# HGRN2 attention and a gated MLP on one core: new group sizes and priorities, and all transposes on TensorE in place of twenty by DMA

## The chip, the cores and the metric

The kernel runs on one core of a Trainium2 chip. The metric is the device time of one execution in microseconds (us), the median of several runs. The kernel before has a median of 213.93 us over 3 runs (213.22 to 216.14).

## What is computed

The inputs are q, k, v and f_logit of shape (4, 8, 768, 48): batch, heads, tokens, head size, all fp32. A gated linear recurrence over the tokens is followed by a two-layer MLP with the activation h * cos(h):

```python
f = 1.0 / (1.0 + np.exp(-f_logit))
for t in range(S):
    state = f[:, :, t, :, None] * state + einsum('bhd,bhe->bhde', k[:, :, t], v[:, :, t])
    y[:, :, t] = einsum('bhd,bhde->bhe', q[:, :, t], state)
x = y.transpose(0, 2, 1, 3).reshape(B * S, H * D)     # 3072 x 384
h = x @ w_in                                          # 384 x 2048
out = (h * np.cos(h)) @ w_out                         # 2048 x 384, fp32
```

## The kernel before

**Chunks.** The 768 tokens of each batch row are cut into chunks of 128, so there are 24 chunks, numbered n = 0 to 23, six to a batch row. Within a chunk the recurrence is done with matmuls, and a state of 48 x 48 per head goes from one chunk to the next of the same row. For every chunk:

- f, k, q and v are loaded by SyncE's DMA queue (`load`, L392-403). The first `NPAIR = 4` chunks put two neighbouring tokens in one partition, in two DMAs of 96 KB (L399), the others take one DMA of 192 KB (L396). The q of chunk 0 is issued by ScalarE's queue.
- `decay` (L413-473) turns f into the cumulated gates: exp (L422) and ln (L437) on ScalarE, cumulated sums by matmuls with a triangle of ones (L448-463), then two exp (L468), which give b and bi. One call serves one chunk or two.
- `attend` (L475-634): qk = q * b and k * bi (L482, GpSimd; VectorE too for n < 4), v cast to bf16 (L389). qk is transposed into qkt. For most chunks this is eight TensorE transposes into one PSUM bank (L511 for paired chunks, L515 for the others) and a copy out of it by VectorE or ScalarE (L525, "qkt"). For n in `TURN_QK` it is one DMA transpose on SyncE's queue (L517), with no PSUM and no copy. Then scores (L541, L550), the causal mask (am, L554, VectorE), the state's product (L570, L575), the state's update (st L584 VectorE, sz L590 GpSimd), y from the state and from the scores (L600, L607, L612), and its cast to bf16 (yb, L525). yb is transposed into xT: three TensorE transposes (L630) and a copy (xT, L525), or for n in `TURN_Y` one DMA transpose on SyncE's queue (L622).
- `moe` (L638-690) works on units of 128, 128, then 256 tokens (`UNITS`): h = xT against w_in (L651, 6 matmuls for each half of a 1024-column PSUM tile), cos on ScalarE (L658), gT = h * cos on VectorE (L661), then w_out (L671, 16 matmuls of 384 columns for 128 tokens), a copy to SBUF (ot, L674) and a store by SyncE (L682, L685).

**Weights.** w_in and w_out come in four pieces each of 768 KB fp32 on SyncE's queue (`load_weights`, L371-386). Each is staged in a slot of the gT pool and cast to bf16 by VectorE, ScalarE or GpSimd (L389), whichever the planner finds free.

**PSUM.** Eight banks serve three kinds of request, whose banks overlap: pairs of banks for h (L350) and for scores (L351), single banks for all else (L352: transposes, y, state products, o). A bank is free for the next request when its last reader is done.

**Who sets the order.** Nothing runs in the order of the Python loops. Each piece of work is an `op` with an engine (or several, with a cost for each), the values it reads and writes, and a priority from the table `PR`. `Plan.run` (L155-245) places the ops one after another on planned engine times: among those that can start about now, the lowest priority number goes first. It thus chooses the engine of every copy and cast, the PSUM bank and buffer of every value, and the order on every engine, SyncE's queue among them. Each engine then executes its list strictly in that order.

`GROUPS` lists the chunks that share a stretch of exp and ln on ScalarE: exp/ln and sin lie in different activation tables, and while a group is open no cosine may be placed. A number is the chunks of one `decay` call. `PR["gate"][g]` holds group g's first exp back until so many cosines are planned:

```python
for o, g in gates:
    if PR["gate"][g] is not None:
        o.deps.add(cosines[PR["gate"][g] - 1])
```

From group 1 (`FREE_GROUPS = 1`) on, the first exp waits until all f pieces of its group are loaded. The table load ahead of an exp group is shown at L737, that ahead of cosines at L658.

Of the kernel before, what the change touches and what calls it, by code (L numbers as in the profile page):

```python
# [116 lines left out]
class Plan:  # L117
# [37 lines left out]
    def run(self):  # L155
# [11 lines left out]
        while len(order) < n:  # L167
# [77 lines left out]
        return order  # L245


GROUPS = [(1, 1, 1), (1,), (2,), (2, 2), (2, 2), (2, 2), (2, 2), (2,)]
UNITS = [128, 128] + [256] * 11
NPAIR = 4  # L250
FREE_GROUPS = 1
TURN_QK = range(14, 23)
TURN_Y = range(12, 23)
PR = {
    "at": [-12.29, -6.15, -7.86, -3.54, -3.92, 15.62, -19.28, -37.09, -8.89, 2.67, 9.58, 17.38, 9.92, 20.25,
          -11.32, -1.58, 13.93, 10.35, 34.42, 26.02, 40.51, 24.64, 16.95, 12.68],
    "dec": [-8.47, -57.31, -61.04, -69.2, -28.24, -49.14, -79.64, -48.44],
    "f": [-43.16, -25.03, -22.97, -8.07, -2.31, -6.19, 24.79, 54.63, 17.72, 57.23, 51.15, 47.24, 55.46,
          53.45, 44.74, 80.64, 54.13, 111.71, 112.22, 68.31, 95.05, 72.38, 86.37, 55.7],
    "h": [3.03, 31.23, 1.72, -0.8, 2.61, 9.56, -7.84, 18.41, -24.77, 18.52, 17.84, 12.56, -12.9],  # L260
    "k": [-21.87, -16.94, -7.69, -4.47, -9.06, 6.14, 15.33, 36.65, 25.42, 15.32, 15.8, 44.24, 49.16, 72.37,
          75.37, 80.56, 68.29, 83.23, 95.28, 87.29, 95.57, 100.98, 97.99, 79.82],
    "o": [58.13, 26.04, 22.05, 54.64, 24.66, 21.51, 44.13, 47.06, 68.58, 102.72, 70.22, 82.65, 82.73],
    "tq": [1.37, -18.62, 8.94, -41.89, -22.72, -30.79, -29.34, 13.32, 0.45, 25.45, 44.49, 73.32, 0.51, 38.11,
          -19.6, -35.07, -26.72, -52.99, -63.88, -22.16, -23.59, 5.62, -39.1, -8.27],
    "ty": [-29.44, -2.23, -1.14, -18.62, -50.77, -26.99, -41.9, -38.55, -40.26, -17.32, 25.61, -2.03, 2.74,
          8.38, 49.55, 45.48, 2.91, -0.4, -39.16, -44.82, -2.61, -2.74, -26.93, -15.21],
    "v": [-26.8, -34.27, -11.26, 0.13, 3.34, 10.3, 16.09, 22.38, 43.81, 38.01, 48.41, 44.56, 41.68, 43.68,
          90.07, 49.48, 98.02, 44.19, 100.52, 65.78, 64.72, 77.22, 79.02, 126.2],
    "w_in": [-45.54, -7.28, 5.66, -12.05],  # L270
    "w_out": [6.72, 10.57, 101.81, 165.61],
    "wc": [0.78, -2, -17.61, -40.6, -45.98, 2.72, 16.43, 45.54],
    "gate": [None, None, 1, 1, 5, 20, 28, 36],
}


def build(nc, cpool, ppool, q, k, v, f_logit, moe_w_in, moe_w_out, out):
# [79 lines left out]
    def act(n, src="P", ptr=False):  # L357
        return 0.833 * n + (160 if src == "P" else 198) + (95 if ptr else 0) - 55

    def dve(n, rate=1.04):  # L360
        return rate * n + 153 - 55
# [113 lines left out]
    def attend(b, c, n, ld, bt, bi, i, prio):  # L475
# [28 lines left out]
        def tr(e):  # L504
# [8 lines left out]
            for j in range(2):  # L513
                for p in range(NP):
                    nc.tensor.transpose(out=o[:, j * NP + p, :], in_=pair(j, p), identity=ident)  # L515
        if n in TURN_QK:
            P.op("tq", {"SP": 420.0}, lambda e: nc.sync.dma_start_transpose(  # L517
# [6 lines left out]
        def cp(e, o, i_):  # L524
            (nc.scalar.copy if e == "ACT" else nc.vector.tensor_copy)(out=o, in_=i_)  # L525
        if n not in TURN_QK:
            P.op("qkt", {"DVE": dve(1024, 0.52), "ACT": act(1024)}, lambda e: cp(
# [92 lines left out]
        x = xT[n]  # L620
        if n in TURN_Y:
            P.op("ty", {"SP": 420.0}, lambda e: nc.sync.dma_start_transpose(out=x.ap, in_=yb.ap),  # L622
# [70 lines left out]
    n, t0, units = 0, 0, list(UNITS)  # L693
    for g, group in enumerate(GROUPS):
        at0 = n
# [74 lines left out]
```

## Time and profile before

| | |
|---|---|
| runs of the kernel | 213.22, 213.93, 216.14 us; median 213.93 |
| the profiled execution | 213.22 us, span of the core 211.4 us |
| granted TensorE clock | 0.984 of full speed |
| busy: TensorE / its weight loads | 174.7 / 130.2 us |
| busy: VectorE / ScalarE / GpSimd | 137.8 / 130.5 / 68.7 us |
| L671 (w_out) and L651 (w_in) matmuls | 70.1 and 69.8 us, 384 and 624 of them |
| L661 (g) / L658 (cosines) / L554 (am) | 57.9 / 52.9 / 29.3 us |
| activation table loads | 14, 1283 ns each |
| DMA | 33.62 MB, mean 159 GB/s; 106560 of 113237 packets under 512 B |
| DMA transposes on SyncE's queue | 9 of qk, 11 of yb |

The span goes from the first to the last instruction of the core; the time of the execution is 1.8 us longer. "Busy" is time in which an engine executed; matmuls overlap, so a matmul's own duration is longer than its share of the path. In the rows of a profile, PE is TensorE, PEld its weight loads, DVE VectorE, ACT ScalarE, POOL GpSimd, and SPq SyncE's DMA queue. L512 is line 512 of the kernel. A row `out<-in` names the tiles by the program's names; all PSUM tiles are called ps. A wait is put down to what ended it.

### The profile page before, as it was taken

To read this page: it belongs to the slowest core of one execution; us is meant where nothing else is said; L and a number is where in the kernel's file an instruction comes from. 1 tells how busy PE (TensorE), PEld (TensorE's weight loads), DVE (VectorE), ACT (ScalarE), POOL (GpSimd) and SP (SyncE) were. 2 spreads that over 40 slices of the span, in tenths; PEclk is the share of its full clock that TensorE was granted. 3 is DMA by queue.
4 is the path that set the end of the run, shared out by engine and by line. 5 is a ranking of instruction groups with operands and counts; after the bars stand their busy time and mean duration, and the time that the engine had idled before them with its cause. 6 is when DMAs were issued, how large, how long until landed. Compare 5 with 4: busy or idle time off the path is not lost.

```text
span 211.4 us, 4701 instructions
## 1 busy us (share of the span) xinstructions
PE 174.7 (83%) x1871; PEld 130.2 (62%) x1871; DVE 137.8 (65%) x179; ACT 130.5 (62%) x157; POOL 68.7 (32%) x108
## 2 busy tenths in 40 slices
PE   0152685678989888999989899999998999989983
PEld 0142574566757745787847657768875678857651
DVE  1825859798858963679882776845896767814400
ACT  2274279867994865295887635689687455815511
POOL 8300114820073134486007751119051711000000
PEclk9999599999999999999999999999999999999999
DMA  6969799999998988979988999845955241011113
GB/s 186 181 168 229 192 228 249 271 245 239 274 180 176 198 169 195 219 167 214 177 170 183 182 221 173 175 128 101 145 111 139 64 86 41 0 52 39 40 39 112
DMA packets 113237, 33.62 MB, mean 159 GB/s; under 512 B 106560, under 2 KB 111680, under 8 KB 113216
## 3 DMA queue, kind: packets, MB, share of 16 engines
q1 hardware_dynamic: 112672, 33.14, 71.8%
q10 hardware_dynamic: 544, 0.20, 0.5%
q8 instruction: 14, 0.23, 0.5%
q14 instruction: 7, 0.06, 0.1%
HBM read 25.17 MB, written 4.72 MB: 141 GB/s over the span
## 4 chain that ended last, share of the span: by engine, by line
PE 50%; DVE 7%; ACT 1%; issue 1%; DVEq 0%; ACTq 0%
PE ps L671 23%; PE ps L651 20%; DVE gT L661 3%; PE ps L612 1%; PE ps L550 1%; ACT ot L674 1%; DVE am L554 1%; DVE st L584 1%; PE ps L458 1%; PE ps L600 1%; PE ps L575 1%; DVE yb L525 1%; DVE qkt L525 1%; PE ps L515 1%; PE ps L630 1%
## 5 line engine op out<-in xcount | busy, mean ns | idle before, releaser
L671 PE MATMUL ps<-w_out_bf,gT 128*128 128x384 bf16 x384 | 70.1, 326 | 6.8 <-DVE st L584 2.1
L651 PE MATMUL ps<-xT,w_in_bf 128*128 128x256 bf16 (+1 forms) x624 | 69.8, 264 | 4.1 <-DVE w_in_bf L389 2.3
L661 DVE TENSOR_TENSOR gT<-ps,cosh 128x1024 bf16<-128x1024 f32 x48 | 57.9, 1219 | 14.7 <-ACT cosh L658 14.2
L658 ACT ACTIVATE cosh<-ps,halfpi 128x1024 bf16<-128x1024 f32 x48 | 52.9, 1113 | 23.1 <-PE ps L651 19.5
L651 PEld LDWEIGHTS <-w_in_bf 128*128 128x128 bf16 x624 | 55.9, 98 | 12.4 <-DVE w_in_bf L389 2.5
L671 PEld LDWEIGHTS <-gT 128*128 128x128 bf16 x384 | 35.6, 97 | 29.0 <-issue 8.5
L482 POOL TENSOR_TENSOR qk<-q,b 128x384 bf16<-128x384 f32 x21 | 21.1, 1004 | 38.1 <-ACT b L468 23.0
L590 POOL TENSOR_TENSOR sz<-st,b 64x192 bf16<-64x192 f32 x32 | 16.1, 503 | 33.1 <-DVE st L584 30.0
L554 DVE TENSOR_TENSOR am<-ps,umask 128x1024 bf16<-128x1024 f32 x20 | 24.4, 1218 | 2.9 <-ACT bi L468 1.3
L482 POOL TENSOR_TENSOR qk<-k,bi 128x384 bf16<-128x384 f32 x20 | 20.4, 1021 | 2.8 <-DMA k<-in_k_dram 2.4
L674 ACT COPY ot<-ps 128x384 f32<-128x384 f32 x16 | 7.7, 478 | 21.8 <-PE ps L671 16.7
L422 ACT ACTIVATE f<-f 128x768 f32<-128x768 f32 (+1 forms) x14 | 10.1, 747 | 9.7 <-DMA f<-in_f_logit_dram 9.6
L468 ACT ACTIVATE b<-ps 128x776 f32<-128x776 f32 (+1 forms) x14 | 10.2, 729 | 8.8 <-issue 4.6
L389 DVE CAST w_in_bf<-gT 128x1536 bf16<-128x1536 f32 x4 | 7.0, 1752 | 9.2 <-DMA gT<-in_moe_w_in_dram 9.2
L584 DVE TENSOR_TENSOR st<-ps,sz 128x384 f32<-128x384 f32 x16 | 8.8, 552 | 5.3 <-PE ps L575 2.4
L525 DVE CAST yb<-ps 128x384 bf16<-128x384 f32 x14 | 7.8, 554 | 6.6 <-PE ps L671 2.1
L389 POOL CAST vb<-v 128x384 bf16<-128x384 f32 x9 | 4.5, 503 | 20.3 <-PE ps L612 16.5
L448 PE MATMUL ps<-sp,incl 128*128 128x384 bf16 x4 | 2.0, 501 | 10.7 <-ACT sp L437 10.7
L468 ACT ACTIVATE bi<-ps 128x768 f32<-128x768 f32 (+1 forms) x14 | 10.1, 723 | 0.7 <-PE ps L511 0.7
L737 ACT ACT_TABLE_LOAD x7 | 9.0, 1283 | 2.2 <-issue 2.1
L437 ACT ACTIVATE sp<-f 128x768 bf16<-128x768 f32 (+1 forms) x14 | 10.0, 744 | 0.1
L389 DVE CAST vb<-v 128x384 bf16<-128x384 f32 x11 | 5.9, 535 | 5.3 <-PE ps L612 5.2
(68 smaller groups left out, 174.5 us busy)
## 6 DMA issues: line engine op xcount, KB each, us to landing
k<-in_k_dram SPq DMA_DIRECT2D x20, 192.0 KB, 4.2
q<-in_q_dram SPq DMA_DIRECT2D x20, 192.0 KB, 4.1
f<-in_f_logit_dram SPq DMA_DIRECT2D x20, 192.0 KB, 4.1
v<-in_v_dram SPq DMA_DIRECT2D x20, 192.0 KB, 3.7
out_dram<-ot SPq DMA_DIRECT2D x20, 192.0 KB, 2.7
gT<-in_moe_w_in_dram SPq DMA_DIRECT2D x4, 768.0 KB, 5.5
gT<-in_moe_w_out_dram SPq DMA_DIRECT2D x4, 768.0 KB, 7.3
f<-in_f_logit_dram SPq DMA_DIRECT2D x8, 96.0 KB, 3.1
```

The costliest lines, as they stand in the source:

```text
L389: (nc.scalar.copy if e == "ACT" else nc.vector.tensor_copy if e == "DVE" else nc.gpsimd.tensor_copy)(out=o, in_=i_)
L422: first = P.op("exp", {"ACT": act(384 * m, "S")}, lambda e: nc.scalar.activation(out=fl(ft.ap), in_=fl(ft.ap), func=AF.Exp, scale=-1.0), r ...
L468: nc.scalar.activation(out=out_.ap[:, 0:m, :], in_=i, func=AF.Exp, scale=s)
L482: lambda e, j=j, src=src, dec=dec: E(e).tensor_mul(out=qk.ap[:, j, :, 0:D].rearrange("p (e h) d -> p h e d", e=2) if pm else qk.ap[:, j, : ...
L525: (nc.scalar.copy if e == "ACT" else nc.vector.tensor_copy)(out=o, in_=i_)
L554: P.op("am", {"DVE": dve(1024)}, lambda e: nc.vector.tensor_mul(out=am.ap.rearrange("p r a n -> p (r a n)").rearrange("p (a n) -> p a n", ...
L584: P.op("st", {"DVE": dve(384)}, lambda e: nc.vector.tensor_add(out=st.ap, in0=pv(), in1=S_in.ap), reads=[ps, S_in], writes=[st], prio=prio)
L590: eng().tensor_mul(out=S_out.ap[s, :, r, :], in0=srcap()[s, :, r, :], in1=bt.ap[s, i, HD:, None].broadcast_to([64, NP, D]))
L651: nc.tensor.matmul(ph.ap[:, g * T:(g + 1) * T], lhsT=w_in_bf[:, m, f0:f0 + 128], rhs=x[:, m, :], start=(g % (G // 2) == 0 and m == 0), sto ...
L658: nc.scalar.activation(out=co.ap, in_=ph.ap, func=AF.Sin, bias=halfpi),
L661: P.op("g", {"DVE": dve(1024)}, lambda e, ph=ph, co=co, gv=gv: nc.vector.tensor_mul(out=gv.ap, in0=ph.ap.rearrange("p (g t) -> p g t", t=T ...
L671: nc.tensor.matmul(po.ap[:, 0:d_model], lhsT=gT.ap[:, j, i * C:(i + 1) * C], rhs=w_out_bf[:, j, :], start=(j == 0), stop=(j == KF - 1))
```

## The change

Only constants at the top of the file change; all functions stay as they are.

- `GROUPS`: the first four chunks form one group, where there were three and one. There are seven groups in place of eight; the calls of `decay` keep their sizes (four of one chunk, ten of two).
- `TURN_QK` and `TURN_Y` become empty: no transposes go by DMA. All 24 chunks take the branches at L520-529 and L625-634.
- `PR`: every priority and every gate has a new value. With them the planner lays down a new order on every engine, and other engines for some copies and casts.

```diff
-GROUPS = [(1, 1, 1), (1,), (2,), (2, 2), (2, 2), (2, 2), (2, 2), (2,)]
+GROUPS = [(1, 1, 1, 1), (2,), (2, 2), (2, 2), (2, 2), (2, 2), (2,)]
 UNITS = [128, 128] + [256] * 11
 NPAIR = 4
 FREE_GROUPS = 1
-TURN_QK = range(14, 23)
-TURN_Y = range(12, 23)
+TURN_QK = range(0)
+TURN_Y = range(0)
 PR = {
...
-    "w_in": [-45.54, -7.28, 5.66, -12.05],
-    "w_out": [6.72, 10.57, 101.81, 165.61],
-    "wc": [0.78, -2, -17.61, -40.6, -45.98, 2.72, 16.43, 45.54],
-    "gate": [None, None, 1, 1, 5, 20, 28, 36],
+    "w_in": [-18.28, -18.39, -16.82, -44.7],
+    "w_out": [15.05, 28.06, 93.44, 75.18],
+    "wc": [11.41, 20.66, 14.9, -38, -7.48, 26.57, 33.33, -29.29],
+    "gate": [None, 1, 1, 9, 28, 1, 40],
```

The other rows of `PR` ("at", "dec", "f", "h", "k", "o", "tq", "ty", "v") change in all their numbers too. In the built program the instructions on the engines differ as follows; those not named are as many as before, though in another order:

| engine | instruction | before | after |
|---|---|---|---|
| TensorE | qk transposes L515 | 88 | 160 |
| TensorE | yb transposes L630 | 39 | 72 |
| VectorE | copies qkt / xT / yb / ot | 9 / 8 / 14 / 8 | 15 / 19 / 8 / 11 |
| VectorE | casts of w_in, of v (whole chunks); qk products | 4, 11; 7 | 1, 10; 6 |
| ScalarE | copies qkt / yb / ot | 6 / 10 / 16 | 9 / 16 / 13 |
| ScalarE | casts of w_in / of w_out | 0 / 1 | 3 / 0 |
| GpSimd | casts of v (whole chunks) / of w_out; qk products | 9 / 0; 41 | 10 / 1; 42 |
| SyncE's queue | DMA transposes | 20 | 0 |

SyncE's queue at the start, before: w_in piece 1, f0, v0, v1, f1, f2, k0, k1, q1, w_in 2, v2, k4, q4, f3, k2, q2, w_in 3, f4, k3, q3, f5, v3, v4, w_in 4, k5, q5, w_out 1. After: w_in 1, f0, f1, f2, v0, k0, k1, q1, v1, w_in 2, w_in 3, w_in 4, k2, f3, q2, k3, q3, v2, f4, v4, v3, f5, k4, q4, v5, k5, q5, w_out 1. (The number is the chunk's.)

## The prediction

> **What bounds the kernel now.** I read the page's busy times and slices first, then a table of busy time by stretch, then the chain of waits, then the timeline of the start. The page:
>
> ```profile
> span 211.4 us, 4701 instructions
> ...
> PE 174.7 (83%) x1871; PEld 130.2 (62%) x1871; DVE 137.8 (65%) x179; ACT 130.5 (62%) x157; POOL 68.7 (32%) x108
> ...
> PE   0152685678989888999989899999998999989983
> ...
> DMA  6969799999998988979988999845955241011113
> ...
> PE 50%; DVE 7%; ACT 1%; issue 1%; DVEq 0%; ACTq 0%
> ```
>
> PE leads, and its idle time lies at the left edge. The DMA engines are nearly full until about slice 28 (148 us). The table by stretch (first PE, weight loads, DVE, ACT and POOL, then clock, DMA share, GB/s) puts numbers on it:
>
> ```profile
> 0.00:57.00 57.00, 31.85 (x430) 26.15 (x431) 38.40 (x59) 34.82 (x47) 17.33 (x41) 0.94 0.94 225
> 60.00:120.00 60.00, 54.18 (x597) 40.12 (x595) 43.53 (x59) 41.44 (x49) 28.39 (x38) 1.00 0.91 186
> 120.00:185.00 65.00, 63.67 (x668) 47.63 (x667) 48.64 (x56) 43.41 (x47) 22.17 (x30) 1.00 0.60 117
> 185.00:212.00 27.00, 22.01 (x150) 14.37 (x147) 5.83 (x5) 8.28 (x12) 0.00 (x0) 0.99 0.16 55
> ```
>
> PE is idle 25.2 us in the first 57, 5.8 us from 60 to 120, and only 1.3 us from 120 to 185. The last is the stretch whose transposes go by DMA. So from 120 us on one more microsecond of PE work is a microsecond of span, and DVE (75%) and ACT (67%) have room. The chain of waits, in order of time, shows at what pace short matmuls really pass:
>
> ```profile
> 102.32 0.45 PE ps L515 x8
> 102.77 0.78 PE ps L671 x4
> ...
> 109.57 0.17 PE ps L630 x3
> ```
>
> A single transpose is listed with 219 ns, but eight of them take 0.45 us of the path and three take 0.17 us: they overlap. The DMA transposes that take their place late in the kernel:
>
> ```profile
> L517 SPq DMA_TRANSPOSE qkt<-qk x9: 1232/1309/2777, 116.0 to 170.0; - x9
> ```
>
> That is 9 of qk; 11 more, of yb, have a median of 1190 ns on SyncE's queue. They land after 3.6 and 2.9 us. The start, from the timeline:
>
> ```profile
> 19.11 1.75 DVE L389 CAST w_in_bf<-gT 128x1536 bf16<-128x1536 f32 x1 [2.42 <-DMA gT<-in_moe_w_in_dram]
> ...
> 22.50 0.52 ACT L422 ACTIVATE f<-f 128x384 f32<-128x384 f32 x1 [3.49 <-DMA f<-in_f_logit_dram]
> ...
> 25.07 0.56 DVE L482 TENSOR_TENSOR qk<-q,b 128x384 bf16<-128x384 f32 x1 [0.32 <-DMA q<-in_q_dram]
> ...
> 27.97 1.75 DVE L389 CAST w_in_bf<-gT 128x1536 bf16<-128x1536 f32 x1 [1.87 <-DMA gT<-in_moe_w_in_dram]
> ```
>
> Each cast or product starts as its transfer lands, so these rows date the transfers: a 768 KB weight piece takes about 3.0 us (27.97 - 25.07, with a little waiting), a 192 KB chunk piece of the paired kind about 1.03 us (the f pieces started exp at 7.56 and 11.68 us, four transfers apart).
>
> **What the Trainium skill says.** TensorE: Matmul & The Clock Gate, "Part 4: PE-mode transpose": a PE transpose goes to PSUM and so needs a copy after it, and took about 275 ns inside one kernel. This trace has 219 ns listed, and 56 ns of pace, which decides. VectorE: DVE Perf Modes, "The three transpose paths": TensorE where PSUM will do, 1309 ns for a 128x128 by DMA. Here one instruction of eight blocks issues in 1309 ns and lands in 3.6 us, so that figure isn't a cost per block here. Perfetto Trace Analysis, "Identifying the Most-Contended Engine": matmul busy time does not tell the distance to roofline. Agreed (weight loads are busy 62%); I use it only to say that PE is never without queued work. The same page, "Optimization Strategy": repeated bubbles can mean that PSUM or SBUF has run out. The waits of PE from 60 to 120 us are of this kind.
>
> **The change part by part.** The title speaks of loads, weights and PSUM, but the pairing of four chunks, the SyncE weight queue and the PSUM code stand in both programs. What differs, by the built order, is this.
>
> *Transposes moved to PE.* TURN_QK and TURN_Y become empty. SP loses 9 + 11 DMA transposes; PE gains 72 + 33 matmuls and as many weight loads. 9 x 0.45 + 11 x 0.17 = 4.05 + 1.87 = 5.9 us, all between chunks 12 and 22, which is from about 105 us on, where PE has no gaps. I take +5.9. Zero would need gaps that aren't there; unpipelined (219 ns each) it would be 23 us, which the chain rows exclude.
>
> *Evictions.* DVE: qkt +6 x 0.69, xT +11 x 0.36, yb -6 x 0.56, ot +3 x 0.55, w_in casts -3 x 1.75, one vb and one qk less (-1.3): -0.2 us in sum. ACT: w_in casts +3 x 1.47 (the row of its one weight cast), minus that one cast, qkt +3 x 1.01, yb +6 x 0.48, ot -3 x 0.48: +7.4. POOL: one qk (1.0), one vb (0.5), one weight cast (about 4 x 0.5, an estimate by elements from the vb row): +3.5 of 68.7. None becomes the bound: ACT would be at 138 of some 217 us. PE's own matmuls hide these; what they can cost is order and banks. 20 more requests for single PSUM banks stand in the late stretch, among those of o, y and ps. PE waits in order, so behind an L671 that waits for an xT copy stands all of PE. From 60 to 120 us, where all transposes go by PE, the table of PE's waits lists 1.3 us of L671 behind xT copies and 0.6 us behind yb copies, 1.9 in 60 us. Over 65 us: +2.1. Bounds: 0 (the order was planned anew) and 5.0 (the whole idle rate of 60 to 120 in place of that of 120 to 185: (5.82/60 - 1.33/65) x 65).
>
> *SyncE's queue.* 9 x 1.31 + 11 x 1.19 = 25 us of issue time fall away, with waits of the queue for qk and yb in which loads and stores stood behind. That is worth little: PE was idle 1.3 us there, so no load was late for it.
>
> *The start.* Chunk 3 joins the first group, and the queue's order changes. The same bytes stand ahead of w_in's second piece, so it lands at 19.1 as before; the third and fourth follow at once, at 22.1 and 25.1 (before: 28.0 and 37.3). Behind them chunk 3's f lands at 27.2 (22.5), chunk 2's q at 28.2 (25.1), its v at 31.3, then three pieces, with chunk 3's v at 34.2. On ACT, which casts the three pieces now: cast of the fourth ends at 26.6; exp and ln of chunk 3 at 28.3; its sums on PE 0.9, b and bi 1.0, table load 1.28: 31.5. First cosine 1.11: 32.6 (before: 33.1). Then comes a cast of chunk 3's v, at the head of ACT's queue, so to 34.7; second cosine, 35.8; table 37.1; exp, ln, sums, b, bi of the next group 3.9 us; table 42.2; six cosines 6.6, two qkt 2.0, a yb 0.5: the next table load is at 51.3, after eight cosines. Before it was at 53.46, after seven. That is 2.2 + 1.1 = 3.3 us ahead. Some 1.3 us of it I expect to lose to small waits among the cosines (the row before had 1.0 beside the one for a weight). So -2.0. Bounds: -5.0 (also without PE's 2.3 us of waits for w_in casts) and +3.0 (chunk 2's q is 3.1 us later, and DVE now has a cast of chunk 1's v, landing near 14.8, ahead of chunk 0's k product, which started at 13.5). Table loads stay seven of each kind, so the merged group saves none.
>
> *Sum.* 211.4 - 2.0 + 5.9 + 2.1 = 217.4 us of span. The profiled execution took 213.22, 1.8 more than its span: 219.2. That execution is 0.7 below the median of the three runs, 213.93; I put the forecast between, 219.5, 2.6% above the median.
>
> **The rivals.**
> *The start pays it back.* The start gains 5.0 and the stalls stay at 1.0: 213.2 - 5.0 + 5.9 + 1.0 = 215.1. For: all of w_in is in place 12 us earlier. Against: PE waited only 2.3 us for its casts, and chunks 2 and 3 come later.
> *Evictions stall PE.* Copies and PSUM banks are what PE waits for late, at the full 5.0, and the start loses 2.0: 213.2 + 5.9 + 5.0 + 2.0 = 226.1. For: ACT has 7.4 us more, and head-of-queue waits for v at 14.8, 31.3 and 34.2. Against: in the kernel before DVE and ACT are under 80% busy in each of these stretches.
> *Faster: the start's idle time is filled.* Of PE's 25.2 idle us before 57, more than 12 vanish because MoE units 0 and 1 run straight through on early weights: 213.2 + 5.9 + 2.1 - 12 = 209.2. It decides from a gain of 11.6 us on (209.6 is 2% under the median). Against: 8.7 of these 25 us precede the first matmul, which waits for f, and f comes no earlier.
>
> **How the numbers follow.** Forecast 0.52 (its own range 217 to 222.5), start pays 0.22, evictions stall 0.20, faster 0.06. Two per cent, 209.7 to 218.2, is about what a measurement of this kernel can tell from no change. Of the forecast's case 0.10 lies under 218.2; so slower 0.42 + 0.20 = 0.62, same 0.10 + 0.22 = 0.32, faster 0.06. The range leaves out the faster case and the ends of the others: 214.5 to 226.
>
> **What would show it.** Right: PE busy near 181 us, idle of 22 to 24 us before 57; eight L515 still at 0.45 us in the chain; the idle of PE after 120 us at 3 to 4 us and ended by copies of xT, qkt or yb; second cosine near 35 us, and eight cosines before the third exp table. The start's step is wrong if PE has done less than 32 us of work by 57, or over 37. The stall step is wrong if the late stretch stays at 1.3 us idle, or goes over 6. The transpose step is wrong if PE's busy time grows by less than 4 us.

## The result, and the profile after

The changed kernel takes 227.2 us in the median of four runs (226.43 to 227.31), beside 215.03 for the kernel before on the same chip: 1.056 times the time, 95% interval [1.047, 1.066]. The forecast was 219.5, with a range to 226. The profiled execution took 227.23 us, with a span of 225.4: 14.0 more than before, where the forecast's sum had 6.0. A profile shows one execution, and that of before (213.22) is the fastest of its four: by the medians the difference is 12.2. So up to 2 of the 14.0 us that follow may belong to the two executions and not to the change.

The lines of the page that answer to those shown of before, with the row of the granted clock:

```profile
span 225.4 us, 4908 instructions
...
PE 187.4 (83%) x1976; PEld 140.9 (62%) x1976; DVE 138.2 (61%) x188; ACT 137.8 (61%) x165; POOL 71.8 (32%) x111
...
PE   0327876699999579799999898989999999998883
...
PEclk9999999679999958999999999999999999999999
DMA  6979899999989999995120189791010100111011
...
PE 58%; DVE 12%; ACT 6%; issue 5%; POOL 0%; DVEq 0%; ACTq 0%
```

PE is busy 12.7 us longer, not 5.9. It has a new hole in slices 14 and 15 (73 to 85 us), and its clock dips twice, to half speed (slices 8 and 9, and slices 15 and 16). The transfers, full until about 100 us, then fall away for some 25 us and come back. DVE and ACT are in the chain with 18% where they had 8%. The table by stretch (columns as in the prediction) is cut, from 57 us on, where the two programs part. First after:

```profile
0.00:57.00 57.00, 35.89 (x415) 28.67 (x416) 35.36 (x60) 31.98 (x41) 19.68 (x42) 0.94 0.93 229
57.00:75.00 18.00, 16.79 (x186) 12.30 (x185) 12.45 (x19) 16.88 (x19) 6.35 (x7) 1.00 0.94 191
75.00:105.00 30.00, 24.98 (x300) 20.15 (x297) 19.56 (x26) 19.54 (x24) 16.02 (x22) 0.89 0.93 189
105.00:225.40 120.40, 109.73 (x1088) 79.74 (x1085) 70.79 (x85) 69.37 (x83) 29.72 (x40) 1.00 0.27 67
```

Then before, with the same cuts; its first row stands in the prediction:

```profile
57.00:75.00 18.00, 16.20 (x168) 11.84 (x165) 13.99 (x19) 13.94 (x18) 7.06 (x8) 1.00 0.92 186
75.00:105.00 30.00, 27.70 (x330) 21.22 (x327) 21.27 (x30) 18.35 (x25) 14.97 (x20) 1.00 0.90 189
105.00:211.40 106.40, 98.96 (x956) 71.03 (x948) 64.17 (x73) 63.35 (x72) 29.30 (x39) 1.00 0.54 111
```

Read the last rows first. At 105 us after has 109.73 us of PE work left where before had 98.96: 10.8 more. From there on PE idles 120.4 - 109.7 = 10.7 us, before 7.4: 3.2 more, with rounding. Together these are the 14.0 us. The added transposes, 105 at 56 ns and all after 105 us, are 5.9 of the 10.8. The other 4.9 I call lag: PE work that before had behind it by then. Most of it is w_out matmuls. Counted from the trace, both kernels have issued 288 L651 by 105 us, but before 100 L671 and after 80; 20 at 0.163 us is 3.3. The rest was not traced to single instructions. At 75 us after had been ahead: 192 L651 in both, and 64 L671 to 56. The lag arises between 75 and 105 us.

### The profile page after: what moved, and what is told of

Same layout as the page of the kernel before. It is cut to its first block, busy times and chain, and to the rows that moved or that the text cites. A ratio compares the mean times of both kernels' runs of the same rounds, so it can differ in the third digit from the quotient of the medians.

```text
span 225.4 us, 4908 instructions
## 1 busy us (share of the span) xinstructions
PE 187.4 (83%) x1976; PEld 140.9 (62%) x1976; DVE 138.2 (61%) x188; ACT 137.8 (61%) x165; POOL 71.8 (32%) x111
## 4 chain that ended last, share of the span: by engine, by line
PE 58%; DVE 12%; ACT 6%; issue 5%; POOL 0%; DVEq 0%; ACTq 0%
PE ps L651 24%; PE ps L671 23%; PE ps L515 3%; PE ps L550 2%; DVE am L554 2%; DVE st L584 2%; ACT qkt L525 2%; PE ps L630 2%; DVE gT L661 2%; DVE qkt L525 2%; PE ps L612 1%; ACT cosh L658 1%; PE ps L600 1%; DVE yb L525 1%; DVE vb L389 1%
## 5 line engine op out<-in xcount | busy, mean ns | idle before, releaser
L671 PE MATMUL ps<-w_out_bf,gT 128*128 128x384 bf16 x384 | 71.3, 328 | 7.2 <-ACT qkt L525 2.5
L651 PE MATMUL ps<-xT,w_in_bf 128*128 128x256 bf16 (+1 forms) x624 | 74.5, 275 | 0.5 <-DVE xT L525 0.4
L651 PEld LDWEIGHTS <-w_in_bf 128*128 128x128 bf16 x624 | 59.1, 102 | 10.1 <-issue 1.0
L671 PEld LDWEIGHTS <-gT 128*128 128x128 bf16 x384 | 35.9, 98 | 29.2 <-issue 9.5
L674 ACT COPY ot<-ps 128x384 f32<-128x384 f32 x13 | 6.2, 479 | 16.4 <-PE ps L671 13.9
L468 ACT ACTIVATE b<-ps 128x776 f32<-128x776 f32 (+1 forms) x14 | 10.1, 729 | 9.6 <-PE ps L461 4.4
L525 DVE COPY qkt<-ps 128x1024 bf16<-128x1024 bf16 x15 | 10.3, 688 | 7.8 <-PE ps L575 2.7
L674 DVE COPY ot<-ps 128x384 f32<-128x384 f32 x11 | 6.0, 554 | 13.2 <-PE ps L671 9.8
L525 ACT COPY qkt<-ps 128x1024 bf16<-128x1024 bf16 x9 | 9.1, 1011 | 7.7 <-PE ps L515 5.4
L525 ACT CAST yb<-ps 128x384 bf16<-128x384 f32 x16 | 7.6, 476 | 9.4 <-PE ps L612 3.9
L515 PE MATMUL ps<-ident,qk 128*128 128x128 bf16 x160 | 12.7, 224 | 0.2 <-ACT ot L674 0.2
L630 PE MATMUL ps<-ident,yb 128*128 128x128 bf16 x72 | 8.8, 237 | 3.9 <-DVE ot L674 1.3
L515 PEld LDWEIGHTS <-qk 128*128 128x128 bf16 x160 | 10.7, 100 | 1.6
```

Of the source, the lines that this page charges most:

```text
L630: nc.tensor.transpose(out=pxv()[:, m, :], in_=yb.ap[:, m * 128:(m + 1) * 128], identity=ident)
L651: nc.tensor.matmul(ph.ap[:, g * T:(g + 1) * T], lhsT=w_in_bf[:, m, f0:f0 + 128], rhs=x[:, m, :], start=(g % (G // 2) == 0 and m == 0), sto ...
L671: nc.tensor.matmul(po.ap[:, 0:d_model], lhsT=gT.ap[:, j, i * C:(i + 1) * C], rhs=w_out_bf[:, j, :], start=(j == 0), stop=(j == KF - 1))
L674: P.op("ot", {"ACT": act(384), "DVE": dve(384)}, lambda e, po=po, ot=ot: (nc.scalar.copy if e == "ACT" else nc.vector.tensor_copy)(out=ot. ...
```

## Experiments

All 18 runs, each with the kernel before on the same chip. Runs named before_... start from the kernel before, all others from the changed kernel, called after. The changed kernel itself stands at 1.056 [1.047, 1.066].

| run | median, us | before | ratio, 95% |
|---|---|---|---|
| before_105 | 219.15 | 214.93 | 1.020 [1.015, 1.025] |
| before_qk_pe | 221.03 | 214.52 | 1.031 [1.026, 1.036] |
| before_v6 | 219.11 | 214.33 | 1.023 [1.019, 1.027] |
| before_v6_pe | 230.82 | 214.33 | 1.078 [1.073, 1.083] |
| after_dma_turn | 231.24 | 214.93 | 1.078 [1.073, 1.083] |
| before_turn_last | 214.88 | 214.40 | 1.000 [0.997, 1.003] |
| before_turn_yb23 | 212.90 | 214.40 | 0.990 [0.987, 0.994] |
| fill_both | 228.12 | 214.93 | 1.063 [1.058, 1.069] |
| fill_late | 229.57 | 214.93 | 1.067 [1.062, 1.072] |
| free_fill | 225.20 | 213.68 | 1.053 [1.048, 1.057] |
| before_start_fill | 215.13 | 214.52 | 1.002 [0.999, 1.004] |
| stores_act | 227.76 | 213.68 | 1.064 [1.059, 1.069] |
| vb22_late | 227.64 | 213.68 | 1.063 [1.058, 1.069] |
| all_three | 228.07 | 213.68 | 1.066 [1.061, 1.070] |
| fill_vb22 | 226.21 | 214.33 | 1.057 [1.052, 1.062] |
| after_gates | 237.34 | 214.33 | 1.099 [1.093, 1.105] |
| after_v6 | 260.28 | 214.52 | 1.210 [1.204, 1.217] |
| after_v6_g12 | 261.23 | 214.52 | 1.218 [1.211, 1.225] |

**The clock.** My first theory after the result was that the two dips cost the missing time. Counted over stretches of 3.41 us, the matmuls of after stream 0.24 of the columns of full speed from 38.2 to 41.6 us and 0.31 from 75.7 to 79.2, and each of these stretches is followed by 6.83 us at half clock. (Full speed is taken as 384 columns in 0.16 us.) Two runs put extra matmuls into these places, fill_both into both and fill_late into the second:

```diff
+    def fill(name, n, o):
+        for _ in range(FILL.get((name, n), 0)):
+            nc.tensor.matmul(o[:, 0:384], lhsT=ident, rhs=w_in_bf[:, 0, 0:384], start=True, stop=True)
...
         def trx(e):
+            fill("trx", n, px.ap)
```

The expectation for fill_both:

> The kernel after, with 32 extra matmuls of 384 columns (results never read) on PE in the two places where its clock fell afterwards: 12 between the transposes of yb of chunk 2 and of chunk 3 (about 38 to 42 us), 20 between those of chunk 6 and of chunk 8 (74 to 82 us). Nothing else is moved. Clock theory ([...] PE's busy time grew by 12.7 and not by 5.9): the clock row has no dip after the first 30 us, busy time of PE without the extra matmuls falls by 5 to 6 us, and the time goes from 227.2 to 221 to 223 although PE has 5 us of matmuls more. Rival (the new order of work costs the time by waits and by the transposes, the clock is a symptom): the extra matmuls fall into gaps at best, 227 to 228, or are added, up to 232.

For fill_late:

> Only the 20 extra matmuls of the second place (74 to 82 us). Clock theory: half of the gain, 224 to 225, the dip near 42 to 48 us stays and the one near 80 to 86 is gone. Rival (waits and transposes): 227 to 230.

What the clock theory said of PE came true; the times are the rival's. (Two of the twenty matmuls for the second place ran at 61 us.) The page of fill_both:

```profile
span 226.1 us, 4972 instructions
...
PE 187.4 (83%) x2008; PEld 140.9 (62%) x2008; DVE 138.4 (61%) x188; ACT 138.0 (61%) x165; POOL 71.7 (32%) x111
...
PEclk9999999999999999999999999999999999999999
```

From its first record at 27.7 us on the clock has no dip, and without the 32 extra matmuls (5.1 us at 0.16) PE is busy 182.3 us, near the forecast's 181. So the rest of after's growth in busy time is half clock. Yet the span is no shorter. The chain of waits says that some extra matmuls were on it:

```profile
76.60 0.65 PE ps L359 x3
...
79.00 0.65 PE ps L359 x3
...
81.63 0.65 PE ps L359 x3
...
82.44 0.49 PE ps L359 x3
...
83.30 0.33 PE ps L359 x2
```

L359 is the line of the extra matmuls. Their bank was itself what PE waited for. (With one more at 61.29 these are 15 and 2.95 us; the next expectation says 18.) So in free_fill they moved to banks with no one ahead of them, and only into waits:

```diff
+FILL = {30: 5, 32: 2, 33: 3, 34: 3, 88: 6, 93: 2, 94: 4, 97: 3}
...
+            if o.eng == "PE":
+                plan.fill(at)
+                at += 1
             o.fn(o.eng)
```

> The kernel after, with 28 extra matmuls of 384 columns put where PE waits (13 from the sums of chunks 4 and 5 to the first L671, 15 between the scores of chunk 7 and the transpose of chunk 8), in a PSUM bank that nobody uses just then, and no more of them than the wait is long. In fill_both 18 of the 32 lay on the chain, 2.9 us, because their bank was itself waited for, so that run did not decide. Clock theory (the two half-clock stretches are on the path): no dip after 30 us, and 222 to 223.5. Rival (the half-clock stretches were hidden, since in fill_both PE had done the same work by 105 us, 286 L651 and 80 L671 against 288 and 80): 226.5 to 228 with the clock at 0.99 or more.

The banks turned out to hold values not yet read, so a part of the hidden units is overwritten (in all_three and fill_vb22 too); every instruction still runs. The span is 223.4, and in place of two dips of 6.83 us there is one of 3.41:

```profile
75.00:105.00 30.00, 27.00 (x333) 20.72 (x330) 21.35 (x29) 20.45 (x24) 15.92 (x22) 1.00 0.92 187
105.00:223.40 118.40, 108.06 (x1062) 78.62 (x1061) 69.14 (x83) 68.43 (x82) 29.71 (x40) 1.00 0.26 66
```

It leaves 1.7 us less work at 105 us and saves 2.0 of span (by the ratios to before it is 0.4%, 0.8 us, and the intervals overlap; the clock theory had 3.7 to 5.2). The run takes away 10.2 of the 13.7 us that after spends in the two dips, which is 5.1 us of PE at full speed, and at most 2.0 came back: most of the half clock fell where PE would have waited anyway.

The start, in the kernel before (before_start_fill; the trace of before has half clock from 20 to 27 us):

```diff
+            nc.tensor.matmul(base["tiles"][0][:, 0:128], lhsT=ident, rhs=umask, start=True, stop=True)
```

> The kernel before with 64 extra matmuls of 128 columns in the waits of the first 22 us (14 ahead of the second sum, 10 ahead of chunk 0's transposes, 40 ahead of chunk 1's state product), in a bank not used before 27 us. If the half clock between 20 and 27 us is on the path: full clock from about 14 us on, and 1 to 2 us less, 212 to 213. If the start waits for transfers anyway: 213.5 to 215.

The time is the same within 0.4%. Full clock lasts from 20.1 us on, not from 27.1, but the trace has a new dip from 37.2 to 44.0 us. That dip need not come from the extra matmuls: before_105 has one from 38.9 to 45.8 us with nothing added there. So whether half clock at the start costs time stays open.

**The transposes alone.** PE transposes of a constant are added in the plan of before (before_105): eight for each of chunks 14 to 22, three for each of chunks 12 to 22.

```diff
         def scores(e):
+            extra(n, 8, 14, sc.ap)
...
         def pey(e):
+            extra(n, 3, 12, py.ap)
```

> The kernel before, its DMA transposes kept, with 105 PE transposes of a constant block added where the changed kernel has its 105 (eight ahead of the scores of chunks 14 to 22, three ahead of the output products of chunks 12 to 22), their results never read. My prediction's term (0.45 us for eight, 0.17 us for three, no gaps to hide in): +5.9 us, about 220. Rival (the gaps between PE's matmuls hide part): +2 to +4. Rival (transposes cost their listed 219 ns): +15 or more.

```profile
105.00:218.20 113.20, 106.73 (x1078) 78.84 (x1074) 65.16 (x76) 65.01 (x74) 29.70 (x40) 1.00 0.47 105
```

The run takes 4.2 us longer by the medians (3.1 to 5.4 by the interval), 6.8 by the spans. The work after 105 us grew by 7.8, of which 2.0 is lag at that point (12 L651, 4 L671) and 5.8 the 102 transposes that come after it: 57 ns each, as the chain had it. The order up to there is that of before but for three transposes, so the 2.0 is a difference between two executions. PE's idle time after 105 us is 6.5 us, 0.9 less than before. So transposes without copies cost their pace or somewhat less: that waits hid a part of it, the first rival, is not excluded by the medians. Nothing beyond the pace shows.

**The transposes with their copies.** In before_qk_pe the qk transposes go to PE in the plan of before, whose PE order stays the same up to chunk 13's output:

```diff
-TURN_QK = range(14, 23)
+TURN_QK = range(0)
```

> The kernel before with qk of chunks 14 to 22 turned on PE (72 transposes and 9 copies), yb of chunks 12 to 22 by DMA as before; PE's order is that of before up to the output product of chunk 13, near 105 us. My terms: 4.05 for the transposes and 9/20 of 2.1 for stalls: +5, about 219. If the copies and the order around them cost as much again as the transposes: +8 to +10, 222 to 224, with PE idle 3 us or more longer after 105 us than in before (7.4). If copies are hidden and gaps take up part: +2 to +4.

```profile
105.00:219.30 114.30, 104.21 (x1035) 76.10 (x1033) 68.95 (x79) 65.53 (x77) 29.03 (x39) 1.00 0.34 78
```

This costs 6.5 us, 3.1%. After 105 us PE has 5.25 us more to do, 4.05 of it transposes by pace; the other 1.2 is mostly work that this execution had not done by 105 us (5 L651 and 8 L550 fewer), though its order up to there is that of before. And PE idles 10.1 us, 2.65 more than before; its longest waits there are state products and L671 behind qkt, yb and ot copies. By the medians, 6.5 less 4.05 leaves 2.45 (1.5 to 3.7 by the interval). So 9 of the 20 copies, with the order that comes with them, cost about what I gave all 20, 2.1, or more. The order changes: 15 cosines now run in one stretch, 117 to 148 us, and two exp groups then follow with one cosine between, where before had groups of eight cosines. The ACT timeline of this run:

```profile
147.85 1.11 ACT L658 ACTIVATE cosh<-ps,halfpi 128x1024 bf16<-128x1024 f32 x1 [0.20 <-PE ps L651]
148.98 1.28 ACT L737 ACT_TABLE_LOAD   x1
...
158.66 1.11 ACT L658 ACTIVATE cosh<-ps,halfpi 128x1024 bf16<-128x1024 f32 x1
159.79 1.28 ACT L737 ACT_TABLE_LOAD   x1
```

After has the same picture (table loads at 124.44 and 135.26 us, 16 cosines ahead of the first). In after the attention of eight chunks, 14 to 21, then comes at once. With both kinds on PE the planner finds an order for the settings of before only with more buffers, hence a pair: before_v6 has six buffers, before_v6_pe has them and both ranges empty.

```diff
-    vS = slots("v", 4, [128, H, D], F32)
+    vS = slots("v", 6, [128, H, D], F32)
-    vbS = slots("vb", 4, [128, HD])
+    vbS = slots("vb", 6, [128, HD])
```

For before_v6:

> The kernel before with six buffers in place of four for v and for its bf16 cast. It is the control for the next run, which needs them. Both theories: 213 to 217, DMA transposes as before.

For before_v6_pe:

> The kernel before with these six buffers and with both ranges empty, so that all chunks turn on PE, with their copies; start, groups, gates and priorities are those of before. If my two late terms were right (5.9 for the transposes, 2.1 for stalls by copies): 7 to 9 us more than the run with six buffers alone. If the copies and the banks are what stalls PE: 12 or more. If the rest of the change (the groups, gates and priorities of after) is what costs the other half: at most 7, and 5 or more better than after.

There are 11.7 us between them (13.2 by the spans): far over my 8.0.

```profile
105.00:216.60 111.60, 103.67 (x1014) 75.36 (x1008) 65.73 (x72) 68.13 (x81) 29.66 (x40) 1.00 0.49 101
...
105.00:229.80 124.80, 112.60 (x1135) 82.89 (x1132) 74.26 (x90) 73.08 (x86) 31.39 (x44) 1.00 0.25 63
```

At 105 us before_v6_pe (the second row) has 8.9 us more PE work left, 5.9 of it the added transposes, and idles 4.3 us longer from there on. The control was to be 213 to 217 and is 219.1: more buffers change the order and cost 2.3% by themselves, so such a comparison of two planned orders carries a few us of its own. The other way round, after_dma_turn gives after the DMA transposes of before:

```diff
-TURN_QK = range(0)
-TURN_Y = range(0)
+TURN_QK = range(14, 23)
+TURN_Y = range(12, 23)
```

> The kernel after with the two ranges of the kernel before, so that chunks 12 and 14 to 22 turn by DMA again; the planner orders the rest anew from the same numbers, which were not made for it. If the 105 transposes on PE are what costs late: 227.2 - 5.9 = about 221, with both clock dips before 90 us still there. If the plan around them is worth more than they are (SyncE's queue has 25 us of issue time more, in a queue that already waits behind stores): 226 or more.

The plan of after is not rescued by DMA transposes: PE is busy 4.2 us less, and idles 46 us where after idles 38. Last, more of them in the kernel before. Both ranges one longer is before_turn_last; the second alone is before_turn_yb23.

```diff
-TURN_QK = range(14, 23)
-TURN_Y = range(12, 23)
+TURN_QK = range(14, 24)
+TURN_Y = range(12, 24)
```

For before_turn_last:

> The kernel before with both ranges one longer, so that chunk 23 turns by DMA too: 11 transposes and two copies fewer on PE, DVE and ACT. By pace: -0.62 us (0.45 + 0.17), 0.3%. If the copies and banks cost as much again: -1 to -1.5. Rival: qk of chunk 23 is needed 2.1 us after its transpose on PE (166.3 to 168.4 us), a DMA transpose lands after 3.6, so PE waits about 1.5 us there or at the end of the chunk: 0 to +2 us.

For before_turn_yb23:

> Only yb of chunk 23 by DMA, 3 transposes and one copy fewer: -0.17 by pace, 0 in what can be measured; xT of chunk 23 is needed 9 us or more after the transpose, so no wait. Rival as above: 0 to +1.

Both together: no difference. Only yb of chunk 23: 1.0% less time than before (0.7 to 1.3% by the interval), the one version that beats both kernels. I expected nothing measurable, and three transposes at 57 ns don't explain 1.5 us. The traces show what else differs: PE's order is that of before up to 180 us, and of three waits of L671 for ot copies by ACT after 105 us, 1.4 us in before, two of 0.57 us (at 189.0 and 204.1 us) are gone. Why the new order needs no such waits, and why both ranges together gain nothing, is open.

**Order, queues, gates.** In after SyncE's queue stands behind stores, and one cast on POOL waits 3.1 us, by my reading for its transfer. The edits: the stores of chunks 4 to 23 on ACT (stores_act); the cast, with the load that takes its buffer, moved behind chunk 13's products (vb22_late); both with the extra matmuls of free_fill (all_three); the cast and the extra matmuls without the stores (fill_vb22).

```diff
-                    nc.sync.dma_start(out=out[r0:r0 + C, :], in_=ot.ap)
+                    nc.scalar.dma_start(out=out[r0:r0 + C, :], in_=ot.ap)
...
+    late = [o for o in order if (o.name == "vb" and o.prio == PR["at"][22]) or o.name == "v15"]
+    order = [o for o in order if o not in late]
+    i = max(j for j, o in enumerate(order) if o.name == "qk" and o.prio == PR["at"][13])
+    order[i + 1:i + 1] = late
```

For stores_act:

> The kernel after, with the stores of chunks 4 to 23 issued from ACT's queue and not from SyncE's; nothing else moved. Theory of the queue's head: in the trace of after, SyncE's queue waits for copies of the output (L674) while loads stand behind it, the DMA share falls from 0.92 to 0.24 between 105 and 120 us and POOL works 2.0 of those 15 us; so with the stores elsewhere the DMA share there is over 0.6, POOL's work is over 5, PE's idle time from 105 to the end falls from 10.7 to about 7, and the time to about 224. Rival (PE has the work it needs there anyway, since it is busy 14.6 of these 15 us, and its order is fixed): the gap in the transfers goes, the time stays at 226.5 to 228, or rises where ACT now waits for copies by DVE.

For vb22_late:

> The kernel after, with one cast on POOL (v of chunk 22, which stands ahead of chunk 10's state product and waits 3.1 us for its transfer in the chain from 93 to 96 us) moved behind the products of chunk 13, and the load that takes its buffer with it. If the order of casts and loads is what holds the stretch from 83 to 105 us: that wait goes, PE has done 6 to 12 more L651 or L671 by 105 us, and 224 to 226. If something else is next in line (transfers that fill the DMA engines at 0.92): 226.5 to 228.

For all_three:

> Extra matmuls in PE's waits, stores on ACT's queue and the late cast together. If the three are separate costs that add up: about 217 to 219, near the kernel before with 105 transposes added (219.2). If one bound stands behind all: no better than the best of the three alone, 224 or more.

For fill_vb22:

> The extra matmuls of free_fill (their bank turned out to be in use, so a part of the hidden units of two chunk pairs is overwritten; the work is unchanged) and the late cast of chunk 22's v, without the stores on ACT, which in all_three were ahead by 3 us at 185 us and behind again at 200. If clock and cast add up: 222 to 223.5. If the gain is swallowed by what comes next: as free_fill, 225.

None gains by its ratio. The first three came out at the rivals' times; fill_vb22, 226.2, keeps little of free_fill's gain (225.2). The late cast is not what holds back the L671: vb22_late has 288 L651 and 80 L671 by 105 us, as after. With the stores on ACT the gap in the transfers stays, so the queue's head is not its cause:

```profile
105.00:120.00 15.00, 14.55 (x146) 10.94 (x144) 11.05 (x14) 6.72 (x10) 2.02 (x4) 1.00 0.26 64
```

POOL works 2.0 us here, as in after. As I read the planned order, the chunks' buffers are held for products that wait for the exp groups at 124 us; no run tests this. all_three had 90 L671 by 105 us, half of the missing twenty, and was 2.2 us of L651 and 0.8 us of L671 ahead of after at 185 us, and by 200 us had the same counts again (575 and 304 to 576 and 304). Where that went is open; stores_act alone also ends late.

Two gates were moved. after_gates (first edit) opens two exp groups earlier. after_v6_g12 (second edit, beside its control after_v6; both have six buffers) lets more cosines run ahead of the exp groups of chunks 10 to 13, to give back the one cosine that after lacks from 75 us on:

```diff
-    "gate": [None, 1, 1, 9, 28, 1, 40],
+    "gate": [None, 1, 1, 9, 20, 28, 40],
...
-    "gate": [None, 1, 1, 9, 28, 1, 40],
+    "gate": [None, 1, 1, 12, 28, 1, 40],
```

For after_gates:

> The kernel after with one line changed: the fourth and fifth group of two times two chunks (14 to 17 and 18 to 21) may start their exponentials after the 20th and the 28th cosine, as in before, and not both after the 28th. The planner orders what follows about 85 us anew. Theory: in after the two groups' attention is bunched behind one visit of the exp table at 124 us (POOL works 2.0 of the 15 us before, then PE waits 4.6 us between 120 and 185), so the split takes 2 to 4 us off: 223 to 225.5, with POOL over 5 us busy between 105 and 120. Rival (a second visit of the exp table costs what the bunching costs, or the priorities don't fit): 227 or more.

For after_v6:

> The kernel after with six buffers for v and its cast, as control for the next. The visit of the exp table for chunks 10 to 13 comes after the 11th cosine, as in after. 225 to 231, and PE waits between 75 and 90 us as in after.

For after_v6_g12:

> The same, with the gate of this visit at the 12th cosine in place of the 9th; the planner then lets 16 cosines run ahead of it. Theory (one missing cosine holds back the outputs of chunks 4 and 5 while the exp table is in use, and PE has nothing to do): more than 100 L671 done by 90 us where after had 64, PE's idle time between 75 and 105 us under 2 us (after: about 5), and 2 to 4 us faster than the run with six buffers alone. Rival (transfers hold this stretch, DMA share 0.92 to 0.98): the L671 come earlier, but chunks 10 to 13 come later by as much, and the time is the same within 1%.

after_gates misses: POOL works 6.5 us between 105 and 120 us as expected, but a new hole of PE opens at 135 to 150 us (9.3 of 15 us busy), and the run is 10 us slower than after. The other pair, at 260 and 261 us, fell apart in its orders (one visit of the exp table lasts from 54 to 77 us there) and says little of after. In it the L671 came no earlier by 90 us, but 103 to 64 were done by 105, with the same time: as far as the pair says anything, it speaks for its rival. So the cause of the lag is read from the traces and not shown by a run.

## Why the prediction was wrong

**The step that failed is the start's, "So -2.0".** It counted a lead at the third exp table load and carried it to the end. The sum had no term for 57 to 105 us. A lead came, smaller: at 75 us after is 8 L671 ahead, 1.3 us. But the table load after the eighth cosine came at 56.99 and not at 51.3. The cosines ahead of it waited for L651, with PE at half clock from 41.6 to 48.4:

```profile
46.87 1.11 ACT L658 ACTIVATE cosh<-ps,halfpi 128x1024 bf16<-128x1024 f32 x1 [1.99 <-PE ps L651]
49.02 1.11 ACT L658 ACTIVATE cosh<-ps,halfpi 128x1024 bf16<-128x1024 f32 x1 [1.04 <-PE ps L651]
...
55.17 1.11 ACT L658 ACTIVATE cosh<-ps,halfpi 128x1024 bf16<-128x1024 f32 x1 [2.22 <-PE ps L651]
...
56.99 1.28 ACT L737 ACT_TABLE_LOAD   x1
```

By 105 us there were 4.9 us of lag in place of the 2.0 of lead: 6.9 of the 8.0 us that the sum missed by the spans, and outside the bound of +3.0. By the medians, 12.2 us apart, the sum missed about 6.

How the lag looks (read from the traces, as said): before runs its twelfth cosine ahead of the exp groups of chunks 10 to 13,

```profile
71.80 1.11 ACT L658 ACTIVATE cosh<-ps,halfpi 128x1024 bf16<-128x1024 f32 x1
72.93 1.28 ACT L737 ACT_TABLE_LOAD   x1
```

after goes to them after the eleventh, and comes back 13 us later:

```profile
69.34 1.28 ACT L737 ACT_TABLE_LOAD   x1
...
82.46 1.28 ACT L658 ACT_TABLE_LOAD   x1
83.76 1.11 ACT L658 ACTIVATE cosh<-ps,halfpi 128x1024 bf16<-128x1024 f32 x1
```

The twelfth completes the hidden units of chunks 4 and 5, so in after no L671 can follow those of chunks 0 to 3. On PE's timeline there is none from 75 to 92 us:

```profile
74.19 0.81 PE L671 MATMUL ps<-w_out_bf,gT 128*128 128x384 bf16 x4 [0.77 <-ACT qkt L525]
...
92.44 0.82 PE L671 MATMUL ps<-w_out_bf,gT 128*128 128x384 bf16 x4
```

Before issued 40 in this time, among them:

```profile
76.08 2.12 PE L671 MATMUL ps<-w_out_bf,gT 128*128 128x384 bf16 x12
78.85 1.46 PE L671 MATMUL ps<-w_out_bf,gT 128*128 128x384 bf16 x8 [0.65 <-DVE ot L674]
...
84.06 2.12 PE L671 MATMUL ps<-w_out_bf,gT 128*128 128x384 bf16 x12
```

A part of this is order only: by 92 us after is 24 L651 ahead of before. But from 75 to 82.9 us PE runs neither kind and is left with attention, in a row of short waits (the table is of 75 to 105 us):

```profile
PE ps L630 <- DVE ot L674: 1.3, 1, 1.3
PE ps L671 <- ACT qkt L525: 1.1, 1, 1.1
PE ps L575 <- DVE yb L525: 0.9, 1, 0.9
PE ps L630 <- ACT yb L525: 0.8, 2, 0.6
```

The clock falls too; free_fill says that its two dips add 2 us to the loss at most.

**Transposes, "+5.9".** Right in the traces, perhaps high in the times: after 105 us eight L515 stand in the chain with 0.45 to 0.61 us, three L630 with 0.17 to 0.34; before_105 has 5.8 for 102 of them in its trace and 4.2 (3.1 to 5.4) by the medians. "PE busy near 181" was wrong as a sign, since half clock adds to busy time; at full clock it is 182.3.

**Stalls, "+2.1".** Right in kind, too small: 3.2 in after, and 2.65 in before_qk_pe with 9 copies of the 20. From 120 to 185 us PE idles 4.6 us (3 to 4 said), behind copies of ot, qkt, xT and yb and state sums. The rate of waits of 60 to 120 us that I took counts copies only; that the whole order shifts, with eight chunks bunched behind two exp groups, was not in it.

**The start's signs.** Second cosine at 34.50 us (35 said), idle time before 57 us 21.1 (22 to 24 said; PE's listed work there contains the first dip), the rest as above. **The rivals:** "evictions stall PE", 226.1, came nearest in time, with the full 5.0 where 3.2 was measured and with a loss of 2.0 at the start where 4.9 was lost later.

**What stays open:** why the planner's order with PE transposes runs 15 or 16 cosines before the next exp group, and how much of the lag would go if the twelfth cosine came first. It is not shown either that the lag at 105 us counts in full at the end: all_three had half of the missing L671 back by then and was no faster than after.

## What to carry to other kernels

Do not carry a lead past the next place where the order changes: compare, stretch by stretch, how much of each kind of work is done by then, not only how busy the engine is. Where a program is laid out by a planner, price a change by its parts in a fixed order first (before_105), and leave room for the new order: here it cost as much again (5.9 us of transposes, 11.7 between before_v6 and before_v6_pe). Two executions of one order differ too: before_105 was 2.0 us behind before at 105 us, so a smaller difference between two single traces says little. Clock dips and busy time are symptoms until a run without them is faster.

## What the runs showed of the hardware

**The clock row begins late.** It shows 9 wherever the trace has no record of the clock, and the first record of after is at 27.95 us, that of before at 16.9. The matmuls say otherwise: in the traces of both kernels, and of every run with such transposes ahead of its first record, transposes in a row start 106 to 107 ns apart there and 56 ns apart after 100 us. So PE starts at half speed, in after until about 28 us. The table's 0.984 for before leaves this out, and the dips above are those after it.

**What stands ahead of a dip.** The Trainium skill, TensorE: Matmul & The Clock Gate, "HAM oscillation — how this bites in real kernels", puts the loss of clock down to gaps of PE over about 3.4 us. The dip of before at 20.3 us goes with such a gap (4.4 us, up to 21.95). The dips of after do not: no gap in the stretches ahead of them is longer than 1.3 us. Short matmuls with waits between them, at 0.24 and 0.31 of the full column rate, were followed by half clock all the same. The traces give no limit for this rate: a stretch at 0.33 was followed by full clock in fill_both (from 41.3 us) and by half clock in stores_act (from 78.1 us), and before_105 lost its clock after one at 0.49 (from 35.5 us).

**What kept it.** In the execution of free_fill 15 matmuls of 384 columns, put into the waits, held the rate at 0.70 to 0.80 from 74.6 to 84.9 us, and the clock stayed full.
